# Two query groups joined in one unit, and the operations up to step 47 written out as one list

## The chip, the cores and the metric

The kernel runs on one core of one Trainium2 chip. The metric is the device time of one execution in microseconds (us). A core has five engines that run at the same time, each taking its own instructions in the order in which the program issued them: PE (matrix products into the memory PSUM), DVE (vector work), ACT (scalar functions and copies), POOL (vector work on SBUF) and SP (here it only issues transfers). They wait for each other through semaphores.

## The reference

Two blocks follow each other. The first is an attention without softmax: two small projections of each query and key are multiplied with each other to 64 features.

```python
batch, n_heads, seq, head_dim = (4, 4, 1088, 32)
r = 8
def phi(x):
    a = np.einsum('rd,bhsd->bhsr', S1, x)
    b = np.einsum('rd,bhsd->bhsr', S2, x)
    return np.einsum('bhsi,bhsj->bhsij', a, b).reshape(*x.shape[:-1], r * r)
q_p, k_p = (phi(q), phi(k))
kv = np.einsum('bhsf,bhsd->bhfd', k_p, v)
z = np.sum(k_p, axis=2)
num = np.einsum('bhsf,bhfd->bhsd', q_p, kv)
den = np.einsum('bhsf,bhf->bhs', q_p, z)[..., None] + 1e-06
attn_out = (num / den).astype(np.float32)
```

The second takes the result as 4352 tokens of width 128 through a layer of width 2048 and back:

```python
h = x @ w_in
g = np.where(h > 0.0, h, 1.0 * (np.exp(np.minimum(h, 0.0)) - 1.0))
return (g @ w_out).astype(np.float32)
```

S1, S2, w_in and w_out arrive as 64-bit floats; the kernel makes 32-bit floats of them with integer operations.

## The kernel before

**Tiling.** A group is eight half tiles of 64 tokens (512 columns); there are eight full groups 0 to 7 and a last half group 8 with the rest of the four batches. w_in and w_out are cut into eight column pairs cp. A step (g, cp) is: mm1 (two halves h = w_in x xg, 512 columns each, L267), elu (ACT: relu L928, exp L930, the functions `elu_a`; DVE: L936, `elu_d`, result gg) and the product with w_out. That product is `mm2` for group 0, `mm2_blocks` for most of group 1, and `mm2_seven` for all others: seven products in place of eight, whose operand sums (`sums7`) POOL forms, and whose weight sums (`weights7`) POOL forms once. After the last pair of a group, `fin_seven_copy`, `fin_seven_a` and `fin_seven_b` add the seven products up, transpose and store. The last half group has its own loop at the end.

**Attention for the groups.** For each batch b: `transp` turns keys and queries (DVE, L291), `KF` or `KF_late` project the keys, `KO` multiplies (kp), `KA` sums over tokens (kv), `Z` and `Z_out` make the sums for the denominator, and `KT_out` sends kv through memory with transfers issued by SP. For queries: `q1` projects (L579), `q2_...` form den and the products qp on DVE, `q4` transposes them, `q5` multiplies with kv (L741; L753 for pairs) and `q5_out` copies the result to xg, the input of mm1. Groups 0 and 1 have versions of their own (`q1_first`, `q4_early`, `q5_early`). Groups 4 and 5, and 6 and 7, form one unit each and share one call; 2 and 3 share q1 but not the rest.

`queries(g5, g1, n)` issues q5 of one unit and q1 of another in one call, writing into the two h tiles of a later step and two others of the tag aux. There are six calls: q1 of 2 and 3; q5 of 2; q5 of 3 with q1 of 4; q5 of 4 with q1 of 6; q5 of 6 with q1 of 8; q5 of 8.

**Weights.** `load_w` brings 64-bit words into raw; the functions `strip`, `floor`, `shift`, `round_s` (DVE, some strips on ACT), `low` (ACT) and `whole` (POOL) turn them into W. `R1(f, i)` applies one of them to the i-th entry of a list: entries 0 to 3 are the halves of pairs 0 and 1, 4 and 5 those of pair 2, and 6 to 10 the pairs 3 to 7. The tag raw has five buffers, shared with the sums of `sums7`.

**Order.** The schedule is manual: each engine runs its instructions in the order of the program. Lines 1014 to 1161 are one such order, written out, for the start and the first five steps. From step 5 on a loop over `steps` issues mm1, the two halves of the elu, and the product of two steps before; the tables `at`, `mid` and `late` put the attention of later groups at places of these steps. h tiles rotate over four buffers of PSUM.

**Loads.** SP issues, in this order: S1, the first part of k of batch 0, the first part of q of batch 0 (tiles 0 to 7), v of batch 0, w_in of pair 0, the second part of q of batch 0 (tiles 8 to 16), w_in of pair 1; `load_rest` then all others. S2 and the second part of k go through ACT's queue.

The start, as it stands before the change:

```python
load_rest()
KO_first(4, 5)
KO_first(5, 7)
KO_first(7, KT)
Z(0, zps, zl)
Z_out(0, zps)
```

Of the kernel before, what the change touches and what calls it, by code (L numbers as in the profile page):

```python
# [29 lines left out]
def kernel(  # L30
# [24 lines left out]
    P = 128  # L55
# [155 lines left out]
    def RA(i):  # L211
        for f in (strip, floor, shift):
            R1(f, i)

    def RB(i):
        R1(low, i)

    def RC(i):
        R1(round_s, i)
        R1(whole, i)  # L220

# [145 lines left out]
    def KF_late(b, n=None):  # L367
        if n is None:
            ps = [psum.tile([P, 512], F32, name="kfps", tag="aux") for _ in range(2)]
        else:  # L370
            ps = hs[steps[n]] = [psum.tile([P, 512], F32, name="h", tag="h", bufs=4) for c in range(2)]
        for c in range(4):
            u, w = divmod(c, 2)
            for g2 in range(2):
                r = slice(64 * g2, 64 * g2 + 64)
                nc.tensor.matmul(ps[g2][32 * c:32 * c + 32, :32 * KT],  # L376
                                 Sxp[r].rearrange("p x c r -> p (x c r)"),
                                 kT[b][r, u * KT:u * KT + KT, 32 * w:32 * w + 32],
                                 skip_group_check=True, tile_position=(64 * g2, 32 * c))
        feats[b] = ps  # L380

    def KF_late_out(b):
        ps = feats[b]
        ab = feats[b] = work.tile([P, 2, KT, H, R], F32, name="abk", tag="abk", bufs=2)
        for g2 in range(2):
            nc.vector.transpose(ab[:, :, :, 2 * g2:2 * g2 + 2, :].rearrange("p x t c r -> p t x (c r)"),
                                ps[g2][:, :32 * KT].rearrange("p (t x y) -> p t x y", x=2, y=2 * R))


# [124 lines left out]
    abw, ans, qp, qpT, xg, xps = {}, {}, {}, {}, {}, {}  # L514
# [47 lines left out]
    units = {g: ([g, g + 1] if 4 <= g < NQ - 1 else [g]) for g in [2, 3] + list(range(4, NQ, 2))}  # L562
# [7 lines left out]
    def q1(g, ps, o, opened):  # L570
        for w in range(4):
# [3 lines left out]
            if g == 2:  # L575
                m, qs = 2 * m, _ap(qs, [[8 * 64, 2], [1, m]])
# [7 lines left out]
    def q1_out_two(rs):  # L584
        if 3 not in abw:
            abw[2, 3] = abw[2][0]
            t = work.tile([P, 2, 4 * H, 4 * R], F32, name="abw2", tag="abw2", bufs=1)
            abw[2], abw[3] = t[:, 0], t[:, 1]
            abw[2, 0] = t
        n = 4 * H // 4  # L590
        for r in rs:
            nc.vector.transpose(abw[2, 0][:, :, n * r:n * r + n, :].rearrange("p g m y -> p g (m y)"),
                                abw[2, 3][r][:, :64 * n].rearrange("p (g m) -> p g m", g=2))

    def q1_out(g):
        (ps, o), n = abw[g], un[g]
        pair = n > 4
        abw[g] = work.tile([P, H * n if pair else H * 4, 4 * R], F32, name="abw", tag="abwp" if pair else "abw",
                           bufs=1 if pair else 2)
        m = H * n // len(ps)  # L600
        for r in range(len(ps)):
# [28 lines left out]

    def q2_den(g):
        q2_prod(g)
        q2_sum(g)
        q2_rec(g)
        q2_an(g)
# [50 lines left out]
    def q5_early_out(g, w):  # L686
# [6 lines left out]
        else:  # L693
# [4 lines left out]
            const.tile([P, 2, 4 * H, 32], F32, name=f"qpE{c}")[:] for c in range(2)]  # L698

# [17 lines left out]
    def q4(g, i=0):  # L717
# [10 lines left out]
        to = qpT[g, i] = exch[(i + (g > 3)) % 2]  # L728
# [17 lines left out]
    def q5_pairs(g, ps):  # L746
        for e in range(2):
            for r in range(4):
                i, o = divmod(un[g] * r, heads(g) * un[g])
                for w in (e, e + 2):  # L750
                    b, t, n = quarter_of(g, w)
                    u = slice(64 * (w // 2), 64 * (w // 2) + 64)
                    nc.tensor.matmul(ps[w][32 * r:32 * r + 32, :64 * n], kv2[b][u, r, :],  # L753
                                     qpT[g, i][u, e, o:o + 2 * n, :], skip_group_check=True,
                                     tile_position=(u.start, 32 * r))
        xps[g] = ps

    def q5_out(g, i=0):

        n = 32 * un[g]  # L760
        ps = xps[g] if len(units[g]) == 1 else xps[g][2 * i:2 * i + 2]
        x = xg[g + i] = work.tile([P, 512], F32, name="xg", tag="xg", bufs=3)
        for w in range(len(ps)):
            nc.scalar.copy(x[:, n * w:n * w + n], ps[w][:, :n])

    def queries(g5, g1, n):

        hs[steps[n]] = [psum.tile([P, 512], F32, name="h", tag="h", bufs=4) for c in range(2)]
        ps = hs[steps[n]] + [psum.tile([P, 512], F32, name="qps", tag="aux") for _ in range(2)]
        if g5 in pairs:  # L770
            q5_pairs(g5, ps)
        elif g5 is not None:
            q5(g5, ps, 0)
        if g1 is not None:
            q1(g1, ps, 256 if g5 is not None else 0, g5 is not None)
        if g5 is not None and g5 not in pairs:
            q5(g5, ps, 1)
# [10 lines left out]
    def seven(g, cp):  # L788
        return 2 <= g < NQ - 1 or g == 1 and cp >= NP - 2

    SS = const.tile([P, 4, NP, 64], F32, name="SS")
    ts, acc, sas = {}, {}, {}

    def weights7(cps):
        a11, a21, a12, a22 = (W[:, cps, 2 * P + 64 * i:2 * P + 64 * i + 64] for i in range(4))
        for i, (x, op, y) in enumerate(((a21, ADD, a22), (SS[:, 0, cps], SUB, a11), (a11, SUB, a21),
                                        (a12, SUB, SS[:, 1, cps]))):
            nc.gpsimd.tensor_tensor(SS[:, i, cps], x, y, op=op)
# [4 lines left out]
    def sums7(g, cp, c):  # L803
        if c == 0:
            ts[g, cp] = work.tile([P, 4, 2, P], F32, name="tt", tag="raw", bufs=5)
        t = ts[g, cp]
        if c == 0:
            return
        b11, b21 = quarter(g, cp, 0, 0), quarter(g, cp, 1, 0)
        us = [[2 * P, 2], [1, P]]  # L810
        nc.gpsimd.tensor_tensor(_ap(t[:, 0], [[4 * P, 2], [P, 2], [1, P]]), _ap(gs[g, cp][:, 0, P:], [[4 * P, 2]] + us),  # L811
                                _ap(gs[g, cp][:, 0], [[P, 2]] + us), op=SUB)
        nc.gpsimd.tensor_tensor(t[:, 1], t[:, 2], b11, op=ADD)  # L813
        nc.gpsimd.tensor_tensor(t[:, 3], b21, t[:, 1], op=SUB)  # L814
# [16 lines left out]
    def mm2_seven(g, cp, first, last):  # L831
# [22 lines left out]
        del gs[g, cp]  # L854
# [9 lines left out]
    def fin_seven_a(g):  # L864
        a, sa = acc[g][0], sas.pop(g)
        uu = work.tile([P, 3, P], F32, name="uu", tag="uu", bufs=1)
        cc = work.tile([P, 4, P], F32, name="cc", tag="cc", bufs=1)
        sas[g] = uu, cc
        if g == 1:
            e = acc[g][1][:].rearrange("p (k s) -> p k s", s=P)  # L870
            nc.vector.tensor_tensor(uu[:, 0], sa[:, 0], e[:, 1], op=ADD)
            nc.vector.tensor_tensor(uu[:, 1:], _ap(uu[:, 0], [[0, 2], [1, P]]), e[:, 2:], op=ADD)
            nc.vector.tensor_tensor(cc[:, 3], uu[:, 2], e[:, 2], op=ADD)
            nc.vector.tensor_tensor(cc[:, 0], sa[:, 0], a[:, :P], op=ADD)
            return
        nc.vector.tensor_tensor(uu[:, 0], sa[:, 1], a[:, :P], op=ADD)
        nc.vector.tensor_tensor(cc[:, 0], sa[:, 0], a[:, :P], op=ADD)

    def fin_seven_b(g):
        b = acc.pop(g)[0 if g == 1 else 1]  # L880
        uu, cc = sas.pop(g)
        pb = b[:].rearrange("p (k s) -> p k s", s=P)
        if g == 1:
            nc.vector.tensor_tensor(cc[:, 1:3], uu[:, 1:], pb[:, 1:3], op=ADD)
            nc.vector.tensor_tensor(cc[:, 3], cc[:, 3], pb[:, 3], op=ADD)
        else:
            nc.vector.tensor_tensor(uu[:, 1:], _ap(uu[:, 0], [[0, 2], [1, P]]), pb[:, 1:3], op=ADD)
            nc.vector.tensor_tensor(cc[:, 2:], _ap(uu[:, 2], [[0, 2], [1, P]]), pb[:, 0:2], op=ADD)
            nc.vector.tensor_tensor(cc[:, 1], uu[:, 1], pb[:, 3], op=ADD)
        ob = work.tile([P, 2, 4, 2, D], F32, name="ob7", tag="ob", bufs=2)  # L890
# [52 lines left out]
    def mm2(g, cp, last, cs=(0, 1)):  # L943
# [5 lines left out]
        for c in cs:  # L949
            quarters(ops[g][:, :n], W[:, cp, (2 + c) * P:(3 + c) * P], gg[:, c, :n],  # L950
                   start=(first and c == cs[0]), stop=(last and c == 1))
# [61 lines left out]

    for t0, t1 in ((2, 5), (KT, KT + 5), (5, KT), (KT + 5, NT)):
# [6 lines left out]
    load_rest()  # L1021
    KO_first(4, 5)
    KO_first(5, 7)
    KO_first(7, KT)
    Z(0, zps, zl)
    Z_out(0, zps)
    keep_warm(1, 96)
    q2_out(0, 1)
    zq = q1z_first()
    make_Sxp()  # L1030
    make_SWs()
    R1(strip, 0, nc.scalar)
    KA_first(range(4, KT), True, False)
    q2_prod(0, zq)
    R1(low, 0)
    q2_sum(0)
    KA_first(range(4), False, True)
    q2_rec(0)
    q2_out(0, 0)
    den_wide()  # L1040
    q4_early(0, 1)
    KS_copy()
    transp(qT, "q", 0, 13, NT)
    R1(strip, 1, nc.scalar)
    q4_early(0, 0)
    R1(floor, 0)
    q4_out(0, 1)
    keep_last(0)
    Z_share(0)
    R1(floor, 1)  # L1050
    KS_turn()
    R1(shift, 0)
    den_turn()
    q4_out(0, 0)
    R1(shift, 1)
    R1(round_s, 0)
    KS_out()
    R1(round_s, 1)
    R1(low, 1)
    q5_early(0)  # L1060
    whole_half(0, 1)
    transp(qT, "q", 0, 8, 13)
    den_out()
    whole_half(0, 0)
    R1(low, 2)
    abwp = q1_second()
    R1(whole, 1)
    q5_early_out(0, 0)
    R1(strip, 2, nc.scalar)
    q5_early_out(0, 1)  # L1070
    mm1_first(0, (0,))
    q1_second_out(abwp)
    R1(strip, 4)
    R1(floor, 2)
    R1(low, 3)
    mm1_first(1, (0, 1))
    R1(floor, 4)
    q2_prod(1)
    R1(strip, 3, nc.scalar)
    q2_sum(1)  # L1080
    R1(low, 4)
    mm1_first(0, (1,))
    q2_rec(1)
    elu_a(0, 0, 1, (0,))
# [278 lines left out]
```

## Time and profile before

| | |
|---|---|
| median of 3 runs | 261.51 us (261.35 to 261.7) |
| profiled execution: its own time | 261.49 us |
| profiled execution: span from first to last instruction | 259.7 us |
| mean granted PE clock | 0.999 |
| PE matmul records | 4115 |
| mm1, 512 columns, 64 wide | 264 records, 592 ns each, 62.3 us busy |
| mm1, 512 columns, 32 wide | 480 records, 592 ns each, 57.6 us busy |
| elu_d on DVE | 128, 684 ns each |
| relu, exp on ACT | 128 each, 590 and 631 ns |
| sums7 on POOL | 50 of each: 1286, 736 and 740 ns |

A matmul of 32-bit floats has two records in the trace, and those of neighbouring columns of the array run at the same time, so that the busy time of a group is far less than its count by its mean. Matmuls overlap; what one costs is read as the time from its start to the start of what follows. DVE's and ACT's records overlap by some 0.1 us with the next one's in the same way. A line such as "DVE gg L936 <- ACT e L930" says who waited, and for whom. One view of waits, before:

```profile
DVE gg L936 <- ACT e L930: 56.4, 74, 1.6
ACT e L928 <- PE h L267: 48.5, 57, 1.8
...
POOL tt L811 <- DVE gg L936: 26.3, 31, 8.2
```

(us in total, times, longest.)

### The profile page before, as it was taken

How to read it: one execution, taken by the hardware profiler on the slowest of the kernel's cores; microseconds unless marked ns; L12 is line 12 of the kernel's file. 1: busy time of each engine (PE TensorE's matmuls, PEld its weight loads, DVE VectorE, ACT ScalarE, POOL GpSimd, SP SyncE). 2: the span in 40 equal slices, each digit the busy share in tenths (PEclk: the TensorE clock that was granted, in tenths of full speed). 3: DMA queues.
4: the chain of work that ended last, by engine and by line, in shares of the span. 5: the costliest groups of instructions: out<-in, count | busy, mean ns of one | idle time of the engine just before them, and what ended most of it. 6: DMA issues, size and time to landing. Idle time of an engine off the chain costs nothing.

```text
span 259.7 us, 9773 instructions
## 1 busy us (share of the span) xinstructions
PE 254.4 (98%) x4115; PEld 157.8 (61%) x4115; DVE 178.9 (69%) x343; ACT 184.9 (71%) x362; POOL 167.7 (65%) x213
## 2 busy tenths in 40 slices
PE   8999999999999999999999999999999999999994
PEld 7742333533346667676666666665666666668993
DVE  6989776896988958997567576743466746544651
ACT  2699878756568677776687777775877777777792
POOL 4634214234279996788688798888688888887310
PEclk9999999999999999999999999999999999999999
DMA  5999990012011211012000204220001110110021
GB/s 171 261 311 294 299 247 23 0 26 89 20 22 25 33 27 23 5 17 35 15 0 3 36 17 105 51 33 10 4 4 28 31 27 3 28 16 3 3 30 33
DMA packets 30379, 15.61 MB, mean 60 GB/s; under 512 B 22496, under 2 KB 28000, under 8 KB 30336
## 3 DMA queue, kind: packets, MB, share of 16 engines
q1 hardware_dynamic: 29904, 14.63, 23.6%
q8 instruction: 32, 0.52, 0.8%
q10 hardware_dynamic: 368, 0.30, 0.3%
q14 instruction: 11, 0.09, 0.1%
q0 software_dynamic: 64, 0.07, 0.1%
HBM read 11.31 MB, written 2.36 MB: 53 GB/s over the span
## 4 chain that ended last, share of the span: by engine, by line
PE 96%; DVE 2%; ACT 1%; issue 0%; DVEq 0%
PE h L267 45%; PE pb L851 17%; PE pa L851 13%; PE o L267 6%; PE pb L827 4%; PE ol L267 3%; PE idle L275 1%; PE kv L458 1%; PE h L741 1%; PE h L579 1%; PE abp L354 1%; DVE kp L427 1%; PE h L753 1%; PE kfps L376 0%; PE qps L741 0%; PE qtp L657 0%
## 5 line engine op out<-in xcount | busy, mean ns | idle before, releaser
L267 PE MATMUL h<-xg,W 128*32 128x512 f32 (+3 forms) x904 | 131.0, 540 | 0.0
L936 DVE SCALAR_TENSOR_TENSOR gg<-e,h 128x512 f32<-128x512 f32 x128 | 87.0, 684 | 59.3 <-ACT e L930 56.4
L928 ACT ACTIVATE e<-h 128x512 f32<-128x512 f32 x128 | 75.3, 590 | 48.6 <-PE h L267 48.5
L811 POOL TENSOR_TENSOR tt<-gg 128x512 f32<-128x512 f32 x50 | 64.3, 1286 | 30.1 <-DVE gg L936 26.3
L930 ACT ACTIVATE e<-e 128x512 f32<-128x512 f32 x128 | 80.6, 631 | 3.7
L267 PEld LDWEIGHTS h<-xg,W 128*32 128x32 f32 (+1 forms) x904 | 42.7, 122 | 42.8 <-issue 34.0
L814 POOL TENSOR_TENSOR tt<-gg,tt 128x256 f32<-128x256 f32 x50 | 37.0, 740 | 3.9
L813 POOL TENSOR_TENSOR tt<-tt,gg 128x256 f32<-128x256 f32 x50 | 36.8, 736 | 3.9
L851 PEld LDWEIGHTS pa<-gg,W 128*64 128x64 f32 (+1 forms) x496 | 23.7, 126 | 22.4 <-issue 22.2
L851 PE MATMUL pa<-gg,W 128*64 128x128 f32 (+1 forms) x496 | 30.6, 274 | 0.0
L142 POOL TENSOR_TENSOR W<-W,raw 128x256 uint32<-128x256 uint32 (+2 forms) x12 | 11.8, 987 | 29.1 <-DVE W L119 28.0
L851 PE MATMUL pb<-tt,SS 128*64 128x128 f32 (+1 forms) x480 | 29.6, 273 | 0.0
L851 PEld LDWEIGHTS pb<-tt,SS 128*64 128x64 f32 (+1 forms) x480 | 22.8, 126 | 0.0
L851 PE MATMUL pa<-tt,SS 128*32 128x128 f32 (+1 forms) x288 | 21.2, 273 | 0.0
L851 PE MATMUL pb<-gg,SS 128*64 128x128 f32 (+1 forms) x256 | 19.9, 273 | 0.0
L851 PE MATMUL pb<-tt,W 128*64 128x128 f32 (+1 forms) x256 | 19.9, 273 | 0.0
L267 PE MATMUL o<-gg,W 128*32 128x512 f32 x128 | 15.5, 595 | 0.0
L851 PEld LDWEIGHTS pa<-tt,SS 128*32 128x32 f32 (+1 forms) x288 | 13.7, 124 | 0.0
L851 PEld LDWEIGHTS pb<-gg,SS 128*64 128x64 f32 (+1 forms) x256 | 12.8, 125 | 0.0
L851 PEld LDWEIGHTS pb<-tt,W 128*64 128x64 f32 (+1 forms) x256 | 12.8, 125 | 0.0
L827 PE MATMUL pb<-gg,W 128*32 128x256 f32 x192 | 11.5, 379 | 0.0
L989 DVE SCALAR_TENSOR_TENSOR gg<-e,h 128x256 f32<-128x256 f32 x16 | 6.6, 418 | 6.4 <-PE h L267 3.2
(169 smaller groups left out, 261.5 us busy)
## 6 DMA issues: line engine op xcount, KB each, us to landing
raw<-in_moe_w_in_dram SPq DMA_DIRECT2D x8, 256.0 KB, 5.9
raw<-in_moe_w_out_dram SPq DMA_DIRECT2D x8, 256.0 KB, 4.6
out_dram<-ob SPq DMA_DIRECT2D x112, 16.0 KB, 1.5
hd_k<-in_k_dram SPq DMA_DIRECT2D x3, 544.0 KB, 9.9
hd_q<-in_q_dram SPq DMA_DIRECT2D x3, 544.0 KB, 11.3
v<-in_v_dram SPq DMA_DIRECT2D x4, 288.0 KB, 10.0
v<-in_v_dram SPq DMA_DIRECT2D x4, 256.0 KB, 10.5
raw<-qpF SPq DMA_DIRECT2D x16, 64.0 KB, 2.0
```

The source lines that it names most:

```text
L142: nc.gpsimd.tensor_tensor(dst.bitcast(U32), dst.bitcast(U32), words(raw)[0], op=ADD)
L267: nc.tensor.matmul(dst[c:c + tile], lhs[:, c:c + tile], rhs, skip_group_check=True, tile_position=(0, c), **kw)
L275: nc.tensor.matmul(idle[c:c + tile, :cols], ones[:, :tile], ones[:, :cols], skip_group_check=True, tile_position=(0, c))
L811: nc.gpsimd.tensor_tensor(_ap(t[:, 0], [[4 * P, 2], [P, 2], [1, P]]), _ap(gs[g, cp][:, 0, P:], [[4 * P, 2]] + us), _ap(gs[g, cp][:, 0], [[ ...
L813: nc.gpsimd.tensor_tensor(t[:, 1], t[:, 2], b11, op=ADD)
L814: nc.gpsimd.tensor_tensor(t[:, 3], b21, t[:, 1], op=SUB)
L827: nc.tensor.matmul(acc[1][0][r:r + width[0], 256 * hi:256 * hi + 256], lhs[:, w:w + width[0]], gg[:, c, 256 * u:256 * u + 256], start=(fir ...
L851: nc.tensor.matmul(bank[r:r + width[0], P * col:P * col + P], lhs[:, w:w + width[0]], rhs[:, u], start=(first and i in ((0,) if g == 1 els ...
L928: nc.scalar.activation(e, hs[g, cp][c][:, :n], RELU, scale=-1.0)
L930: nc.scalar.activation(e, e, EXP, scale=-1.0)
L936: nc.vector.scalar_tensor_tensor(gs[g, cp][:, c, :n], es[g, cp][:, c, :n], -1.0, hs[g, cp][c][:, :n], op0=ADD, op1=MAX)
L989: nc.vector.scalar_tensor_tensor(gs["last", k // 2][:, k % 2, :2 * P], es["last", k // 2][:, k % 2, :2 * P], -1.0, hs["last", k][:, :2 * P ...
```

## The change

1. Groups 2 and 3 become one unit, as 4 with 5 and 6 with 7 are. `q1_out_two` goes; `q5_out` copies one quarter per call. `queries` takes lists: a call can hold several q5 and q1, side by side in the same tiles. There are five calls: q1 of 2; q5 of 2; q1 of 4 and of 8; q5 of 4 with q1 of 6; q5 of 6 and of 8. The last half group's products use tiles of their own (`qpE2`, `xgl`).
2. `sums7`, `weights7`, `fin_seven_a`, `fin_seven_b` and `KF_late_out` issue one instruction per call, so that the list can place them singly; the transposes of k and q of batches 1 to 3 are cut in two.
3. The tables and the loop up to step 47, group 5's last, are replaced by one written list of some 830 operations in another order. From group 6 on the loop stays. Loads are issued where they were.

```diff
-    units = {g: ([g, g + 1] if 4 <= g < NQ - 1 else [g]) for g in [2, 3] + list(range(4, NQ, 2))}
+    units = {g: ([g, g + 1] if g < NQ - 1 else [g]) for g in range(2, NQ, 2)}
...
-    def queries(g5, g1, n):
+    def queries(g5s, g1s, step):
...
+        hs[step] = [psum.tile([P, 512], F32, name="h", tag="h", bufs=4) for c in range(2)]
+        ps = hs[step] + [psum.tile([P, 512], F32, name="qps", tag="aux") for _ in range(2)]
+        sums = [(g, 256 * i) for i, g in enumerate(g5s)]
+        keys = [(g, 256 * i) for i, g in enumerate(g1s, len(g5s))]
+        for g, c in sums:
+            if g in pairs:
+                q5_pairs(g, ps, c)
+            else:
+                q5(g, ps, 0)
+        for g, c in keys:
+            q1(g, ps, c, c > 0)
+        for g, c in sums:
+            if g not in pairs:
+                q5(g, ps, 1)
...
     load_rest()
+    R1(low, 0)
+    R1(strip, 0, nc.scalar)
+    R1(low, 1)
+    Z(0, zps, zl)
+    transp(qT, "q", 0, 13, NT)
     KO_first(4, 5)
+    KO_first(7, KT)
     KO_first(5, 7)
-    KO_first(7, KT)
-    Z(0, zps, zl)
+    KA_first(range(4, KT), True, False)
+    transp(qT, "q", 0, 8, 13)
     Z_out(0, zps)
+    R1(strip, 1, nc.scalar)
+    zq = q1z_first()
+    KA_first(range(4), False, True)
+    KS_copy()
+    q2_out(0, 1)
+    q2_out(0, 0)
+    q4_early(0, 1)
+    q2_prod(0, zq)
+    R1(floor, 0)
+    q2_sum(0)
+    q4_early(0, 0)
+    q4_out(0, 1)
+    q2_rec(0)
+    R1(shift, 0)
+    R1(floor, 1)
+    den_wide()
+    q4_out(0, 0)
...
+    KS_turn()
+    KS_out()
+    abwp = q1_second()
+    den_turn()
+    q5_early(0)
     keep_warm(1, 96)
...
     den_out()
+    q5_early_out(0, 0)
+    q5_early_out(0, 1)
+    q1_second_out(abwp)
+    mm1_first(0, (0,))
...
+    mm2(0, 1, False, (0,))
+    mm2(0, 1, False, (1,))
+    R1(floor, 7)
+    elu_a(1, 0, 1, (0,))
+    elu_a(1, 0, 1, (1,))
+    elu_d(1, 0, 1)
+    R1(floor, 5)
+    elu_a(1, 0, 0, (0,))
+    elu_a(1, 0, 0, (1,))
+    R1(shift, 7)
+    R1(shift, 5)
+    elu_d(1, 0, 0)
+    R1(round_s, 5)
+    R1(low, 8)
+    elu_a(0, 2, 1, (1,))
+    R1(low, 5)
+    R1(low, 6)
+    R1(whole, 5)
+    mm1(1, 1, (0,))
+    mm1(1, 2, (1,))
+    transp(kT, "k", 1, 9, NT)
     elu_d(0, 2, 1)
+    R1(strip, 8)
+    transp(kT, "k", 1, 0, 9)
+    mm1(1, 2, (0,))
...
```

## The prediction

> **What bounds the kernel now.** I read the page's head first, then the chain that ended last, then the timeline of the first 20 us, and last the groups of instructions for the price of single operations.
>
> ```profile
> span 259.7 us, 9773 instructions
> ...
> PE 254.4 (98%) x4115; PEld 157.8 (61%) x4115; DVE 178.9 (69%) x343; ACT 184.9 (71%) x362; POOL 167.7 (65%) x213
> ...
> PE   8999999999999999999999999999999999999994
> ...
> PE 96%; DVE 2%; ACT 1%; issue 0%; DVEq 0%
> ```
>
> PE is full in every slice but the first and the last. Busy matmuls can hide waits, so I took start to next start: an mm1 of a full step takes 1.717 us wherever it stands, an mm2_seven 1.528, from 28 us to the tail, without a hole. The only part of the span that is not PE at its pace is the start, which the chain of waits shows:
>
> ```profile
> 7.54 1.48 DVE kp L427 x3
> 9.34 0.75 DVE qp L644
> 11.11 0.62 ACT denw L664
> 12.93 0.75 DVE W L119 x2
> 14.16 0.88 PE abwp L552 x16
> 15.04 3.58 PE h L267 x48
> ```
>
> Until the first mm1 (its first matmul starts at 14.97) DVE, ACT and PE take turns on one chain: products of batch 0 (kp), key sums, first query group, xg. From 14.97 to its last matmul's end at 255.96 PE is dense, except for 0.42 us at 18.55 (eight qtp transposes take 1.28 us to the next start; at 0.107 us each they are 0.86). Then 3.7 us of output. So the span is start 14.97, plus PE work, plus tail. The change can win only PE work, that 0.42 us, or an earlier start; each wait that it adds at PE costs its full length.
>
> **The change at the start.** The new list puts transp(qT, 0, 13, NT) on DVE ahead of the three KO_first; before, it came after both q2_out(0). It reads the second part of query batch 0. The timeline of the first 16 us shows that load's issue and its neighbours:
>
> ```profile
> 3.96 0.61 SPq L188 DMA_DIRECT2D raw<-in_moe_w_in_dram  x1
> 4.61 0.57 SPq L81 DMA_DIRECT2D hd_q<-in_q_dram  x1
> ...
> 6.50 0.70 DVE L291 STREAM_TRANSPOSE qT<-hd_q 128x512 f32<-128x512 f32 x1
> ...
> 7.54 1.70 DVE L427 TENSOR_TENSOR kp<-abp,abk 128x256 f32<-128x256 f32 x3 [0.34 <-ACT abk L362]
> ...
> 9.85 0.44 ACT L129 ACTIVATE W<-raw 128x256 f32<-128x256 f32 x1 [0.57 <-DMA raw<-in_moe_w_in_dram]
> ...
> 11.54 0.45 DVE L291 STREAM_TRANSPOSE qT<-hd_q 128x256 f32<-128x256 f32 x1
> ```
>
> ACT waited until 9.85 for the weights issued at 3.96; the query part was issued behind them on the same queue. The trace's packets of it run from 8.32 to 10.04, and its semaphore's last step is at 10.62. At 11.54 the old order found it there. The diff moves no load. DVE works its queue in order, so in the new order it stands from 7.20 to about 10.65, and KO_first stands behind it. [...]
>
> I lay the new order on the engines with the rows' durations; consecutive DVE operations start some 0.09 us before the end of the one ahead. DVE: transpose at 10.65, next start 0.35 later; KO_first 0.41, 0.61 and 0.68, so they end at 12.70, before 9.24: 3.46 late. Then transpose 0.42, Z_out 0.14, two q2_out 0.70 and 0.55, product 0.20, floor 0.20, sum 0.33, reciprocal 0.25: to 15.40. ACT: denw 0.62, q4_out 0.48, KS_out 0.28, to 16.73. PE: q5_early 0.67 with its issue; DVE: xg 0.43, to 17.88. First mm1 at 17.95 for 14.97: **+2.98**. Behind the blocked transpose wait KA_first on PE, KS_copy on ACT and everything above; POOL's KO_pool runs free. ACT's early low(0), strip, low(1) wait for weights until 11.2 but nothing due earlier is behind them. Bounds: landing at 9.85 gives +2.2, at 11.54 +3.9.
>
> **After the start.** h has four buffers, so mm1(1,2) takes over that of mm1(0,2)'s second half, which elu_d(0,2,1) frees. That half's exponential now stands behind the elus of (1,0) and low(8). PE reaches mm1(1,2) after: mm1_first 1.72, mm1(0,1) 1.83, q4_early 0.91, mm1(0,2) 1.83, q5_early 0.62, mm2, mm1(1,0) and mm2 5.16, a half mm1 0.86 = 13.0, at 30.95. ACT from 17.40: three low at 0.46, two strip at 0.35, query copies 1.9, the relu and exp of seven halves and one more relu (0.48 to 0.63 and 0.54) 8.4, low(8) 0.70, one wait for PE 0.2, the late exp 0.54 = 13.8, to 31.2. DVE's queue comes to elu_d(0,2,1) after a 512-column transpose at 31.77 and ends it at 32.4. PE waits **+1.45**. Bounds: nothing (these sums leave out half-overlaps I can't see), and 2.9, twice it. Before, DVE and ACT were as full here, but the old order freed this buffer at 25.55:
>
> ```profile
> 20.00:30.00 10.00, 10.00 (x112) 3.09 (x108) 9.53 (x22) 9.26 (x19) 3.49 (x4) 1.00 1.06 311
> 30.00:40.00 10.00, 10.00 (x132) 3.73 (x128) 6.56 (x12) 6.75 (x12) 2.15 (x3) 1.00 0.92 218
> ```
>
> (Columns: window, its us; busy PE, PEld, DVE, ACT, POOL; clock; DMA.) A sum of the whole new list by these durations puts DVE and ACT level with PE for the first 16 us of PE work, 2.6 and 0.9 us ahead after 22, 4.0 and 6.3 after 33, and further ahead later. Weights of column pair 7 load when whole(5) frees a buffer, some 8 us later than now (24.66), and land near 41, just before strip(10) wants them. For such local waits on the rest I take **+0.3** (0 to 2).
>
> **Queries.** PE time of the six calls, start to next start: 0.66, 1.00, 1.63, 2.06, 1.46, 0.52 = 7.33; around each some 0.14 goes on the change of shape (the mm1 ahead takes 1.83 for 1.717, the matmul behind 0.03 more). After, five: q1(2) 0.66; q5(2) at 256 columns, 2.06 - 0.66 = 1.40; q1(4) with q1(8) 0.66 + 0.39; q5(4) with q1(6) 2.06; q5(6) with q5(8) 1.06 + 0.52: 6.75. With one change of shape less: **-0.7**. The 1.40 is the row nearest; 1.00 and 2.00 (128 columns once and twice) bound it. The q4_early wait at 18.55 goes, since both q2_out(1) end before PE is there: **-0.42**, or nothing if it only moves.
>
> DVE and ACT save a few instructions on group 3, hidden under PE. Singly listed sums7, weights7, fin_seven and halved transposes issue the same work; their cover is PE's dense stretch, where DVE, ACT and POOL stand at 60 to 85%.
>
> **Sum:** 2.98 + 1.45 + 0.3 - 0.7 - 0.42 = +3.6: span 263.3. The profiled run took 261.49, 1.8 us around its span, and the median is 261.51, so the time is **265.1 us**.
>
> **Rivals.** A, *the load is there in time* (not slower): if it lands by 7.2, when DVE comes free, the transpose fills DVE's 0.34 us gap, the start stays near 14.97, and with no buffer wait the sum is -0.7 - 0.42 = -1.1: 260.4. It decides where the landing is before some 8.7, at which the slip eats the 1.1. Against it stand ACT's wait to 9.85 and the packets: 0.05. B, *only the start slips*: ACT and DVE overlap better than my sums, no buffer wait and no local ones: 265.1 - 1.75 = 263.4. For it: PE never waited there before; against: the exp moved behind four elus. 0.22. C, *PE cools*: PE now has nothing from 8.94 (Z's end) to 11.45, then short pieces; the granted clock read 1.00 throughout, with gaps below 0.8 us after its first matmul. Were it to halve for two mm1, they would take 3.4 us more: 268.5; 0.08. [...] D, *the new order waits more later*: orders are in strict sequence per engine, and 800 entries have many places; 2 us more: 267.1; 0.15. The forecast has 0.50.
>
> Range 263.0 to 267.6: it takes in B, D and the bounds of the landing, and leaves out A and C. Within 0.2% (0.5 us, about what a measurement tells from no change) needs A with part of the slip: 0.02. Faster 0.05, slower 0.93.
>
> **What would show it.** Right: DVE idle from 7.2 to 10.6 before a qT transpose, released by the query load; kp at 11.0; first h matmul near 18; a PE wait of 1 to 2 us for elu_d near 31; then steps at 1.717 and 1.528. Wrong: kp still at 7.5, a first h matmul before 16, PE without a wait at 31, or a clock below 1.00 in the first windows.

## The result and the profile after

| | before | after |
|---|---|---|
| median | 261.63 us (261.35 to 262.85, 6 runs) | 269.81 us (268.44 to 270.84, 6 runs) |
| profiled execution: span | 259.67 | 267.90 |
| first matmul of mm1 starts | 14.97 | 20.43 |
| from there to the end of PE's last matmul | 240.99 | 243.84 |
| from there to the end of the span | 3.71 | 3.63 |

The ratio is 1.0309, 95% interval 1.0286 to 1.0332: slower by 8.2 us, where the prediction had 3.6 and ended its range at 267.6. The direction was right, the size was not. The page of the changed kernel, its head and chain:

```profile
span 267.9 us, 9634 instructions
...
PE 256.0 (96%) x4051; PEld 160.9 (60%) x4051; DVE 176.5 (66%) x345; ACT 181.9 (68%) x357; POOL 165.9 (62%) x213
...
PE   8499999799999989999999999999999999999994
...
PEclk9779999999999999999999999999999999999999
...
PE 92%; DMA 2%; issue 2%; SPq 1%; DVE 1%; ACT 0%; DVEq 0%
```

Before, PE was full from the second slice to the last but one. Now the second slice is at 4, the eighth at 7 and the fifteenth at 8; the granted clock falls to 0.7 of full in the second and third slice; and the chain's share of "issue", time in which an engine waits for nothing that the profile shows, is 2% where it was 0%. The three marks are three different losses.

**The start.** The chain of waits in its first 21 us:

```profile
4.59 6.04 DMA hd_q<-in_q_dram
...
11.02 1.59 DVE kp L414 x3
...
12.66 1.08 PE kv L431 x32
13.74 1.00 PE zqp L530 x16
14.74 1.01 PE kv L431 x32
15.75 1.85 PE qtp L628 x8
```

DVE stands for the second query load before that (the last bracket is the idle time before, and who ended it):

```profile
10.65 0.45 DVE L280 STREAM_TRANSPOSE qT<-hd_q 128x256 f32<-128x256 f32 x1 [2.64 <-DMA hd_q<-in_q_dram]
```

kp starts at 11.02, as forecast. Behind it the pieces on PE last up to twice what they did: zqp 1.00 (before 0.59), 32 matmuls of kv 1.01 (before 0.51 for as many, 72 taking 1.14), qtp 1.85. The two rows of the kernel before, behind which its next group started at 11.12:

```profile
9.39 0.66 PE L543 MATMUL zqp<-SW,qT 128*64 128x32 f32 x16
9.98 1.21 PE L444 MATMUL kv<-kp,v 128*32 128x64 f32 x72
```

A window of the changed kernel's start says why (columns: window, its us; busy PE, PEld, DVE, ACT, POOL; clock; DMA share, GB/s):

```profile
10.60:17.40 6.80, 5.19 (x96) 4.54 (x97) 6.12 (x17) 1.84 (x6) 0.81 (x2) 0.50 0.83 256
```

The clock was halved from 10.59 to 17.4, for 6.8 us. Of the slip of 5.46 us, the forecast 3.0 of standing would leave 2.5 to the half clock; experiment 2 measures 3.41 and 2.05.

**Two stops.** The timeline of PE near 47 and near 98 us:

```profile
45.80 0.81 PE L802 MATMUL pb<-gg,W 128*32 128x256 f32 x8
48.53 0.84 PE L802 MATMUL pb<-gg,W 128*32 128x256 f32 x11 [1.91 <-issue]
```

```profile
97.12 0.31 PE L445 MATMUL kv<-kp,v 128*32 128x64 f32 x5
98.77 0.27 PE L445 MATMUL kv<-kp,v 128*32 128x64 f32 x4 [1.34 <-issue]
```

PE stops in the middle of a group of matmuls, and no semaphore ends the wait. Summed from each start to the next start, the groups in which it happens grew from 10.36 to 13.26 us (mm2_blocks, 192 records) and from 3.35 to 4.93 (KA, 216 records): 4.48 us, of which the two gaps are 3.25. The page counts 32 packets of a queue named "instruction", of 16,384 bytes each, in both kernels; one of them moved near each stop, from 45.76 to 46.79 and from 96.44 to 97.31. That gave the theory for the first experiments: PE stops because its next instructions are not there.

What is left of the difference is PE work saved: 2.85 - 4.48 = -1.6 us from the first mm1 on. The sum: 5.46 + 4.48 - 1.6 - 0.1 = 8.2.

### The profile page after: what moved, and what is told of

It is laid out like the page before. It is cut to its first block, busy times and chain, and to the rows that moved or that the text cites. A ratio compares the mean times of both kernels' runs of the same rounds, so it can differ in the third digit from the quotient of the medians.

```text
span 267.9 us, 9634 instructions
## 1 busy us (share of the span) xinstructions
PE 256.0 (96%) x4051; PEld 160.9 (60%) x4051; DVE 176.5 (66%) x345; ACT 181.9 (68%) x357; POOL 165.9 (62%) x213
## 4 chain that ended last, share of the span: by engine, by line
PE 92%; DMA 2%; issue 2%; SPq 1%; DVE 1%; ACT 0%; DVEq 0%
PE h L256 44%; PE pb L826 16%; PE pa L826 12%; PE o L256 5%; PE pb L802 4%; PE ol L256 3%; DMA hd_q<-in_q_dram 2%; PE kv L445 1%; PE qtp L628 1%; PE kv L431 1%; PE h L564 1%; PE h L713 1%; DVE kp L414 1%; SPq L81 0%; PE xps L653 0%
## 5 line engine op out<-in xcount | busy, mean ns | idle before, releaser
L925 DVE SCALAR_TENSOR_TENSOR gg<-e,h 128x512 f32<-128x512 f32 x128 | 85.0, 679 | 65.6 <-ACT e L919 47.7
L256 PE MATMUL h<-xg,W 128*32 128x512 f32 (+2 forms) x776 | 120.9, 584 | 0.3 <-DVE xg L665 0.3
L919 ACT ACTIVATE e<-e 128x512 f32<-128x512 f32 x128 | 78.7, 630 | 2.8
L256 PEld LDWEIGHTS h<-xg,W 128*32 128x32 f32 (+1 forms) x776 | 35.7, 119 | 46.7 <-issue 31.0
L826 PEld LDWEIGHTS pa<-gg,W 128*64 128x64 f32 (+1 forms) x496 | 24.6, 126 | 22.7 <-issue 22.3
L256 PE MATMUL o<-gg,W 128*32 128x512 f32 x128 | 16.1, 594 | 0.0
L802 PE MATMUL pb<-gg,W 128*32 128x256 f32 x192 | 13.2, 381 | 1.9 <-issue 1.9
L802 PEld LDWEIGHTS pb<-gg,W 128*32 128x32 f32 x192 | 6.4, 110 | 8.3 <-issue 5.2
```

What stands on the lines that cost most here:

```text
L256: nc.tensor.matmul(dst[c:c + tile], lhs[:, c:c + tile], rhs, skip_group_check=True, tile_position=(0, c), **kw)
L802: nc.tensor.matmul(acc[1][0][r:r + width[0], 256 * hi:256 * hi + 256], lhs[:, w:w + width[0]], gg[:, c, 256 * u:256 * u + 256], start=(fir ...
L826: nc.tensor.matmul(bank[r:r + width[0], P * col:P * col + P], lhs[:, w:w + width[0]], rhs[:, u], start=(first and i in ((0,) if g == 1 els ...
L919: nc.scalar.activation(e, e, EXP, scale=-1.0)
L925: nc.vector.scalar_tensor_tensor(gs[g, cp][:, c, :n], es[g, cp][:, c, :n], -1.0, hs[g, cp][c][:, :n], op0=ADD, op1=MAX)
```

## The experiments

Each was run beside the kernel before; the ratio is to that, with its 95% interval in square brackets. Round brackets behind a median hold the fastest and the slowest run. "After" is the profiled run of the changed kernel.

**1. The two late transposes back behind the start chain.**

```diff
-    transp(qT, "q", 0, 13, NT)
     KO_first(4, 5)
...
-    transp(qT, "q", 0, 8, 13)
     Z_out(0, zps)
...
     KS_copy()
+    transp(qT, "q", 0, 13, NT)
...
     KS_out()
+    transp(qT, "q", 0, 8, 13)
     abwp = q1_second()
```

> The changed kernel with the two transposes of queries 8 to 15 (tiles 13:NT and 8:13) put back behind the start chain, 13:NT behind the copy KS_copy and 8:13 behind KS_out, nothing else. Theory (VectorE's stand at the load, and TensorE's half clock that follows from the gap, together cost 5.46 us): first mm1 near 15.0 instead of 20.43, granted clock 1.0 throughout, time near 264.3 (269.8 less 5.5). Rival 1 (the stand costs the 3.0 of the prediction, and the half clock comes from the new order whatever VectorE does): first mm1 near 17.4, half clock still there, time near 266.8. Rival 2 (the order of the list waits for something else further on, and takes the start's gain back): 268 or more, with the first mm1 near 15.

Median 267.51 (265.71 to 269.09), ratio 1.0226 [1.0162, 1.0290]; the profiled run took 266.14. The clock stayed at 1.0 through the start, but the first mm1 came at 17.00, not 15.0: the place I chose was too late for its reader, and PE stood 1.37 us before q1_second for DVE's qT. Both stops are there, 2.18 us at 43.2 and 0.76 at 94.3. The moved line and the half clock belong together; the size was not settled by this run.

**2. PE kept busy in the gap.** `keep_warm(5)` ahead of the transpose, nothing else.

> The changed kernel with five idle matmuls of 256 columns on TensorE (about 0.43 us each) in the gap in which it waits for VectorE; the stand at the load stays. Theory (the gap is what lowers the clock): the clock stays at 1.0, the pieces of the start chain take their former time, first mm1 near 17.95 instead of 20.43, time near 267.3. Rival (the clock goes down for another reason, or the 5.46 us are all wait): first mm1 within 0.5 of 20.43 and time within 0.7 of 269.8.

```profile
8.79 2.44 PE L264 MATMUL idle<-const-float32-1.0 128*128 128x256 f32 x10
11.50 0.32 PE L431 MATMUL kv<-kp,v 128*32 128x64 f32 x8 [0.27 <-DVE kp L414]
...
18.38 0.85 PE L256 MATMUL h<-xg,W 128*32 128x256 f32 x12 [0.34 <-DVE xg L665]
```

kv starts where it did (11.50 for 11.46), so the wait for kp is the same; the clock stays at 1.00, and the first mm1 is at 18.38 instead of 20.43. The gap makes the half clock, and that costs 2.05 us. The time hardly moved all the same: median 269.78 (267.72 to 270.45), ratio 1.0288 [1.0244, 1.0333]. The gain went into the first stop, now 3.00 us, and into a half clock behind it:

```profile
46.95 0.22 PE L422 MATMUL kv<-abk 128*32 128x32 f32 x1 [3.00 <-issue]
```

The stop is in front of another matmul than before. Counted in PE's matmul records it is at the same place: 600 records lie ahead of it in the changed kernel, in experiment 1 and here, where ten of the 600 are the records of the added idle matmuls; and 1490 lie ahead of the second stop in all three. The stop belongs to a place in PE's instruction stream, not to an operation.

**3. The one line alone, in the kernel before.**

```diff
+    transp(qT, "q", 0, 13, NT)
     KO_first(4, 5)
```

(and taken away behind KS_copy).

> The kernel before with one line moved: the transpose of queries 13:NT from behind KS_copy to ahead of KO_first(4, 5), where the changed kernel has it. Theory (this line alone makes the whole loss at the start): first mm1 20.4 instead of 15.0, half clock for one or two stretches of 3.4 us, time near 267.1 (261.6 plus 5.5). Rival (the prediction's term, a plain stand of 3.0 with no change of clock): 264.6. Rival (the loss needs the rest of the new order too): under 263.

Median 265.35 (265.29 to 266.34), ratio 1.0154 [1.0131, 1.0177]: 3.65 us, between the plain stand and both losses. The first mm1 is at 19.13 for 14.97, which is 4.16. In this order PE stands 3.52 us for Z_out's SW and then runs at half clock from 12.40 for about 3.4 us, one stretch instead of two. No stop follows.

**4. Column tiles of 64 for 32**, which makes 3231 matmul records of 4051.

```diff
-    width = [32]
+    width = [64]
```

> The changed kernel with column tiles of 64 from the start of the program where it has tiles of 32 up to step 31 (width = [64]): the same products in half as many instructions of the same summed time. Theory (the stops of 1.9 and 1.3 us with no releaser near 47 and 97 us are TensorE waiting for its instructions): they go, as the instruction queue moves fewer blocks than 32 and each block lasts longer; time near 265.5 (269.8 less 3.2 for the two gaps and up to 1.2 of slower pace beside them). Rival (the stops belong to data or to semaphores that the profile doesn't show): time within 0.7 of 269.8 and the stops still there.

Median 266.79 (266.20 to 267.69), ratio 1.0203 [1.0176, 1.0230]: 3.0 us less than the changed kernel, with the first mm1 still at 20.14. No stop is left behind the start. The queue moved 25 packets instead of 32.

**5. Wide tiles in the kernel before**, a control.

> The kernel before with column tiles of 64 from the start, nothing else: a control for the run of the changed kernel with tiles of 64, which was 3.0 us faster than with 32. Theory (the width matters through the instruction stream alone, and the kernel before has no stop in it): 261.6 within 0.6. Rival (tiles of 64 are quicker by themselves): 259.5 or less. Rival (they are slower by themselves, their summed time hiding it): 262.5 or more.

Median 262.73, ratio 1.0042 [1.0029, 1.0054]. The second rival holds: wide tiles are slower by about 1.1 us in a kernel that has no stop. They help the changed kernel in spite of that, so the stops cost it about 4 us, not 3, if the tiles cost as much there. Why they are slower was not tested.

**6. Six raw buffers instead of five.** In the changed kernel SP stands 14.5 us at the load of the last weight pair (the view of SP's waits: us in total, times, longest):

```profile
SPq L188 <- POOL W L142: 14.5, 1, 14.5
```

It waits for whole(5) on POOL, and the loads of keys, values and queries stand behind it. Then they run from 36 to 48.5 us; before, the DMA share was 0.06 from 39 to 48.5.

```diff
-tag="raw", bufs=5)
+tag="raw", bufs=6)
```

(in both places that use the tag).

> The changed kernel with six buffers for the raw weight pairs in place of five, so that the load of the last pair, which stands ahead of the loads of keys, values and queries of batches 2 and 3 on SP, doesn't wait for whole(5) on GpSimd (35.2 us). Theory A (the stop at 46.6 us is a fetch of TensorE's instructions that comes late behind these loads, which fill the DMA engines from 36 to 48.5 us): the loads end near 40 us, as before the change, the stop near 46 is gone, the one near 97, where few loads run, stays; time near 267.6 (269.8 less 1.9 and a little pace). [...]

Median 267.44 (266.23 to 267.97), ratio 1.0208 [1.0178, 1.0239], 0.2 us from theory A's number. Windows with the columns of the start, the changed kernel first, then this run:

```profile
42.00:44.00 2.00, 2.00 (x38) 0.77 (x32) 1.84 (x3) 1.51 (x4) 1.55 (x2) 1.00 1.09 240
44.00:46.00 2.00, 2.00 (x107) 1.76 (x101) 1.08 (x3) 1.94 (x5) 0.00 (x0) 1.00 1.01 352
46.00:48.00 2.00, 0.62 (x9) 0.11 (x1) 1.31 (x4) 1.24 (x3) 0.00 (x0) 1.00 1.05 225
```

```profile
42.00:44.00 2.00, 2.00 (x38) 0.76 (x32) 1.83 (x3) 1.51 (x4) 1.55 (x2) 1.00 0.04 11
44.00:46.00 2.00, 2.00 (x107) 1.78 (x101) 1.07 (x3) 1.94 (x5) 0.00 (x0) 1.00 0.00 0
46.00:48.00 2.00, 2.00 (x44) 1.58 (x39) 2.00 (x6) 1.28 (x3) 0.00 (x0) 1.00 0.03 8
```

PE's counts are the same to 46 us; the share of the DMA engines is 0.04 and less instead of 1.01 to 1.09, and PE goes on. The instruction packet there moved from 42.74 to 43.82 instead of 45.76 to 46.79. The second stop stays (1.06 us at 95.1).

**7. The query load ahead of the values.**

```diff
+    load_hd(nc.sync, "q", q, 0, 8, NT)
     load_v(0)
     load_w(0, 0)
-    load_hd(nc.sync, "q", q, 0, 8, NT)
```

> The changed kernel with one load issued earlier: queries 8 to 15 of batch 0 ahead of the values of batch 0 on SP. Theory (VectorE's stand is the landing at 10.6 us and nothing else): the queries land near 7.8, VectorE doesn't stand, the values land near 9.9 instead of 8.9, first mm1 near 16, granted clock 1.0, time near 265.4. Rival (the values become what the start waits for, and TensorE's gap stays as long): first mm1 at 18 or later, half clock again, 267.5 or more.

```profile
8.74 0.45 DVE L280 STREAM_TRANSPOSE qT<-hd_q 128x256 f32<-128x256 f32 x1 [1.32 <-DMA hd_q<-in_q_dram]
...
11.09 0.77 PE L431 MATMUL kv<-kp,v 128*32 128x64 f32 x40 [2.46 <-DMA v<-in_v_dram]
```

The rival holds for the start: DVE still stands 1.32 us, kp starts at 9.11, but PE waits 2.46 us for the values instead, to 11.09, the clock halves at 11.94, and the first mm1 is at 18.41. The stops are 3.00 and 1.06 us. Median 266.72 (265.25 to 268.75), ratio 1.0169 [1.0130, 1.0207], under the rival's 267.5. In this list the start waits for whichever of the two loads comes later; the order before does not need the second query part so early.

**8. Three undoings at once**, with q1_second moved too.

```diff
-tag="raw", bufs=5)
+tag="raw", bufs=6)
...
-    width = [32]
+    width = [64]
...
     KS_copy()
+    transp(qT, "q", 0, 13, NT)
...
     q5_early(0)
+    transp(qT, "q", 0, 8, 13)
+    abwp = q1_second()
```

(and each of the three calls taken away where it stood).

> The changed kernel with three undoings at once: the transposes of queries 8 to 15 and the products q1_second that read them back behind the start chain (13:NT behind KS_copy, 8:13 and q1_second behind q5_early(0)), column tiles of 64 throughout, six raw buffers. Theory (start 5.46 and instruction fetch 3.2 to 4.5 are all of the loss, and some 1.7 us of TensorE work is saved underneath): first mm1 within 0.7 of 15.0, no stop over 0.5 us behind it, time 260.5, so 0.3 to 1.6 under the kernel before. Rival 1 (the list waits elsewhere once TensorE comes earlier): 262.5 or more with the start near 15. Rival 2 (the start still slips, as in the first undoing, at another reader of the late queries): first mm1 at 16.5 or later, 262 or more.

Median 262.91, ratio 1.0043 [1.0027, 1.0059]. No stop, clock 1.0, first mm1 at 16.27: something of the start was still lost (0.68 us before kv for Z_out, 0.72 before denp for denw), close to rival 2's 16.5, and the wide tiles may cost what experiment 5 showed.

**9 to 11. The start in the order of the kernel before**, all its operations up to the first mm1, then with six raw buffers, then with the second burst split:

```diff
     KA(3, (0,))
-    KA(3, (1,))
     mm1(2, 5, (1,))
...
     mm1(2, 4, (1,))
+    KA(3, (1,))
```

(zls[3] and KT_out(3) move with it.)

> The changed kernel with the whole start, from the loads to the first product of mm1, in the order of the kernel before (all its operations, nothing else moved). Theory (the start costs 5.46 us and the two fetch stops stay): first mm1 at 15.0, clock 1.0 there, stops near 41 and 92 us, time 264.3. Rival (TensorE arrives earlier and the list waits elsewhere): 266 or more with the first mm1 at 15.

Start at 14.98, as expected. Times from 264.41 to 267.05, median 265.74, ratio 1.0155 [1.0106, 1.0204]; the fastest of them, at clock 1.00, is 0.1 us from the theory. The stop at 41.6 lasts 2.20 us, and in the profiled run (266.46) the clock halves behind it:

```profile
42.00:44.00 2.00, 0.16 (x4) 1.00 0.55 126
44.00:46.00 2.00, 2.00 (x24) 0.50 0.03 8
```

(Columns: window, its us, busy PE, clock, DMA.) The second stop, 1.06 us, is at 94.4.

> The same with six raw buffers besides. Theory: the loads no longer pause, the stop near 41 us goes, the second one (some 1 to 1.3 us, near 91) stays: 261.9. Rival (with the start undone the loads and the fetch meet at another place): 263 or more.

Median 262.46, ratio 1.0040 [1.0017, 1.0063], 0.6 over the expectation. No stop at 41 us, though mm2_blocks still takes 11.15 us, 0.8 more than before the change; the second stop stands, 1.34 us at 89.8.

> The same again, with the second half of KA(3), a burst of 36 small products and their Z tiles, placed two half mm1 (0.86 us each) further back. [...] Rival (the second stop isn't the burst): the stop stays at 1 us or more, 261.9.

Times from 261.60 to 266.11, without a usable interval: inconclusive as a time. Its trace is not:

```profile
43.22 1.07 PE L802 MATMUL pb<-gg,W 128*32 128x256 f32 x16 [1.71 <-issue]
...
96.91 0.64 PE L826 MATMUL pb<-tt,SS 128*32 128x128 f32 x16 [0.55 <-issue]
```

The burst runs through: KA's 216 matmuls take 3.35 us, exactly as before the change. The stop that was behind 1491 matmul records is now behind 1619, 128 later, in another operation, and down to 0.55 us. The first stop is back, though: loads still ran (DMA share 0.19 from 40 to 42 us, 0.02 in experiment 10), and the instruction packet began at 40.89, in experiment 10 at 38.32. Up to there the two kernels are the same. In experiment 10 it moved while the share was still 0.50 (38 to 40 us; 0.63 here), and here only in the 2 us with 0.19: the share of the loads alone does not settle when the packet moves, and what else does is open.

**12 and 13. Without any stop.** Experiment 10 with wide tiles throughout; and experiment 11 with wide tiles only to mm2_blocks(2, (1,)), behind which `width[0] = 32` stands.

> The changed kernel with the start in the order before, six raw buffers and column tiles of 64 throughout. Theory (no block of instructions is then used up faster than the next comes; the wide tiles cost about 1 us, as in the control on the kernel before): no stop over 0.6 us behind the start, first mm1 at 14.6 to 15.0, time 261.5. Rival (something besides start and fetch holds the list): 262.5 or more without a stop in the trace.

Median 262.52, ratio 1.0020 [0.9988, 1.0052]. No stop, first mm1 at 14.74. That is 1.0 over the theory and the rival's case: 262.5 without a stop.

> The changed kernel with the start in the order before, six raw buffers, the second half of KA(3) further back, and column tiles of 64 only up to mm2_blocks(2, (1,)), near 43 us. Theory: the block of instructions at the first stop lasts twice as long, so that the fetch behind the loads comes in time, and the split keeps the second stop under 0.6; time 260.8, 0.7 under the kernel before. Rival (half the instructions further ahead move the block ends, and another burst meets one): a stop over 1 us at a new place, 262 or more.

Median 261.99 (261.25 to 264.58, 12 runs), ratio 1.0015 [0.9986, 1.0044]. No stop behind the start; first mm1 at 14.86, from there to PE's end 241.06, the kernel before has 240.99. Forecast was 260.8. With the start and the stops out, the change is worth nothing that can be measured. From start to next start, the query calls, q4_early and mm1 save 1.3 us here; mm2, mm2_blocks and KA take 1.0 more than in the kernel before, smaller groups the rest. How much of that the wide tiles cost was not separated. No version beat the kernel before.

## Why the prediction was wrong

**DVE's stand: right in its mechanism, 3.41 us for 2.98.** kp came at 11.02, and with the clock held (experiment 2) the first mm1 at 18.38, 0.4 later than forecast. (The working has ACT at 16.73 where 15.40 and 1.38 make 16.78; its 17.88 fits the latter.) Experiment 9, with the order of the start put back, has it at 14.98: nothing else delays the start.

**"PE cools": set aside wrongly, about 2 us of the error.** It stood as a rival at 0.08, priced for two mm1; the kernel before, with gaps below 0.8 us behind its first matmul, gave nothing to price it by. The gap did halve the clock, in the start chain and not in mm1. Experiment 2 prices it at 2.05 us. The clock fell 1.66 us after the end of PE's last matmul (8.93 to 10.59) and stayed at half for 6.8 us. In experiments 2, 3, 7 and 9 it stayed there for about 3.4 us, and by their windows and timelines it fell some 4.0, 3.4, 3.3 and 2.4 us after PE's last matmul ahead of the gap. What sets the moment is not shown.

**Waits after the start: the step that failed most.** The prediction laid engine against engine and buffer against buffer, found PE's stretch "without a hole" in the kernel before, and put +0.3 on the rest. It had no term for the instruction stream. The runs showed 4.48 us there. The number of the 16,384-byte packets on the queue "instruction" goes with PE's records: 32 packets for 4115 matmul records and as many weight loads before the change, 32 for 4051 after it, 30 for 3907 in experiment 13 and 25 for 3231 in experiment 4, which is 253 to 260 records a packet. From that I estimate a block of some 127 matmuls with their weight loads per packet; no view shows what a packet holds. The stops lie 890 matmul records apart, seven such blocks, whatever operation stands there, and are gone with column tiles of 64. Near the first, the packet came late while data moved: 127 matmul records ahead of the stop PE is at 42.46 us in the changed kernel and at 42.48 with six raw buffers, and the packet begins at 45.76 with a DMA share of 1.06 in between, and at 42.74 with 0.04; experiment 11 shows that the share is not all of it. The second is a burst: with KA's small products among them, 0.016 us each from start to start, the 127 records ahead of the stop take 2.7 us (94.74 to 97.43), and PE goes on 4.0 us after the start of the first of them; with the burst split, the stop falls to 0.55. Why the second packet begins only 1.70 us behind that start is open: the DMA share was 0.27 in between, and no run tested it.

The prediction saw the delayed loads ("some 8 us later than now") and asked only whether their data came in time. They did: behind the first mm1 PE has no idle time but the two stops. Their price shows at the first stop, where the instruction packet began 3.0 us later than in experiment 6.

**The buffer wait near 31 us: wrong, it is zero.** The sum had +1.45, with mm1(1, 2) taking over the buffer that elu_d(0, 2, 1) frees. PE and DVE at that place:

```profile
32.66 2.76 PE L256 MATMUL h<-xg,W 128*32 128x512 f32 x24
```

```profile
34.53 0.65 DVE L925 SCALAR_TENSOR_TENSOR gg<-e,h 128x512 f32<-128x512 f32 x1
```

elu_d(0, 2, 1) ends at 35.18, 2.8 us later than forecast, and PE ran on from 32.66 without a gap, mm1(1, 2) among it. That matmul used a buffer that was free already: the h tiles share four buffers, but not in strict rotation, which was my assumption. By luck the wrong term made the forecast look nearer than its right ones were: without it they give 263.6.

**Queries and q4_early: nearly right.** Forecast -0.7 and -0.42; PE's query calls went from 7.33 to 6.73 us, q4_early's eight transposes from 1.28 to 1.02. The products of mm1 went from 118.4 to 117.3, of which the forecast had only one change of shape. All that PE saved behind the first mm1 is 1.6, 0.5 more than forecast.

The miss of 4.7 us adds up: +0.4 for the stand, +2.05 for the clock, +4.2 for the stops (4.48 for 0.3), -1.45 for the buffer, -0.5 for the work saved.

**Rival A** asked for the load by 7.2, and saw its limit at some 8.7. Experiment 7 brought it to 8.74, and the start moved by only 2.0 us, since the values then came late.

## What to carry to other kernels

When an order is changed, read the start for operations that now stand ahead of a load, and price the clock that an idle PE loses as well as the wait: of the 5.46 us here, 2.05 and 3.41. In a kernel that is bound by PE, count instructions as a resource too. Here PE stopped for 1.34 us in a burst of matmuls of 0.016 us each, and for 1.91 us while the loads held the DMA engines at a share of 1.01 to 1.09, both times with no releaser in the profile. Look for "issue" in the chain and for the same count of records ahead of the stop in two variants.

## What the hardware showed that I had not expected

- The length of a gap did not settle whether the clock fell. It was halved around gaps at the start of 2.53 us (changed kernel), 2.46 (experiment 7) and 3.52 (experiment 3), in experiment 4, where no matmul ran from 9 to 11 us, and behind stops of 2.20 (experiment 9) and 3.00 us (experiment 2); behind stops of 1.91 (changed kernel), 2.18 (experiment 1) and 3.00 us (experiment 7) it was not. So a stop can cost twice: experiment 9 took 264.41 at a mean clock of 1.00 and 266.46 with 0.994, experiment 1 took 265.71 and 266.14 at 1.00, 269.09 and 268.89 at 0.994 and 0.991. In the changed kernel and in experiment 7 the times follow the clocks only loosely.
- The instruction packets of 16,384 bytes took 0.9 to 1.6 us each in the kernels before and after, and at the two stops PE went on 1.74 and 1.46 us after the end of one. Counted from the place 127 matmul records ahead of the stop, the packet began 3.30 us later at the first stop (DMA share 1.06 in between) and 1.70 us later at the second (0.27); in experiment 6, where the first stop was gone, 0.26 us later (0.04 from 42 to 44 us).
- Column tiles of 64 instead of 32 made the kernel before slower by 0.42%, although they make fewer instructions (3295 matmul records for 4115) and an mm1 takes 1.72 us from start to next start with either width.
